# Routing constants ahead of the gate load, one group's transposes one unit later, last transposes ahead of logits

## The chip, the cores and the metric

The kernel runs on one NeuronCore of a Trainium2 chip. The metric is the device time of one execution in microseconds; the time shown is the median of three runs. The engines are named as in the profile: PE (TensorE, matmuls and transposes) with its weight loads PEld, DVE (VectorE), ACT (ScalarE), POOL (GpSimd), and SP (SyncE), whose queue issues almost all DMAs.

## The reference

Windowed attention over 4 batches of 576 tokens with 8 heads of 64, then a mixture of 8 experts with a fixed capacity of 288 tokens each, then a second MLP with a squared ReLU.

```python
# attention: 64-wide causal window
scores = scale * np.matmul(q, k.transpose(0, 1, 3, 2))
mask = (rel >= 0) & (rel < window)
attn = softmax(np.where(mask, scores, -1e9))
out = np.matmul(attn, v)
...
# moe: all (token, expert) logits in descending order; a token goes to its first expert with room
logits = x @ w_gate
for idx in np.argsort(-logits.flatten()): ...
out[mask] = np.maximum(x[mask] @ w1[e], 0.0) @ w2[e]
...
# moe2
h = np.maximum(x @ w_in, 0.0)
return (h * h @ w_out)
```

The order of all logits decides who gets which expert, so the first expert can start only when attention is through for every token.

## The kernel before, in words

Attention works on 18 units. A **group** n (0 to 5) is a third of the sequence (192 tokens) of two batches; each group has three units j of 64 queries. The units run in the order (0,0), (0,1), (0,2), (1,0) and so on, and step s of the main loop is a software pipeline over them:

- `scores` of unit s on PE (32 matmuls into the PSUM tile `sp`, of which there is one), then the masked maximum on DVE and the exponentials on ACT into `P` (`exps`);
- `ptr_` of unit s-1: PE transposes `P`, ACT copies the result to `PT`;
- `pump(s)`: the SP queue issues loads that fall due;
- `xtr` of unit s-2: transposes its output `X` for the gate logits;
- `pv` of unit s-1: 32 matmuls of `PT` with the value tiles `w`, then the division on DVE into `X`; a group's last unit also stores `X` to DRAM (`xs`);
- in every third step `logits` (gate logits of a whole group) and `turn` (they are transposed into `L`);
- `tr(n,h,p)`: a quarter of a group's keys and queries (batch h of the pair, head half p) is transposed on PE, 4 transposes of `kn` and 4 of `qn`, each of these into one of the four small PSUM tiles `pt`; DVE copies the keys to `KT`, ACT the queries to `QT`. The table `due` says in which step which quarter is transposed. Group 0 is done ahead of the loop, amid matmuls on the identity (`keep_warm`).

Keys and queries are loaded by `load_qk`, 8 DMAs for a group (16 half ones for group 0), each of 192 KB in pieces of 256 bytes; the order of all loads on SP is fixed by the list `loads`, and a load of SP has to wait for the semaphore of the eighth load ahead of it. For blocks that overlap, POOL copies half a value tile from the tile before (line 66).

`Routing.constants` (called through `between`) makes what the router needs: on POOL six iotas, two clears of 128x2304 half-precision tiles (`G`, `A_`, lines 295 and 296) and a triangle; on DVE one scaling of `tab` (line 293), which reads what POOL's iota wrote, and six small clears. Before, it is called at the end of step 6.

After attention come eight routing phases (DVE and PE in turn), which find each expert's tokens; the first gives the expert number that the first weight load waits for. The expert and MLP matmuls follow in an order that is fixed when the program is built.

Of the kernel before, what the change touches and what calls it, by code (L numbers as in the profile page):

```python
# [18 lines left out]
def A(t,off,dims):  # L19
    return bass.AP(tensor=t.tensor, offset=t.offset+off, ap=[list(d) for d in dims])  # L20

def attention(tc, nc, q,k,v,wgate, xs, L, identf, between=lambda: None, before_last=lambda: None, WARM=(8,4,4,4), NW=14):


    with ExitStack() as st:
# [12 lines left out]
        units=[(n,j) for n in range(6) for j in range(3)]  # L38
        N=len(units)
# [37 lines left out]
        def pump(s):  # L77
            while loads and loads[0][0]<=s:
                o,n,x=loads.pop(0)
                if x is None: load_qk(n)  # L80
                else: load_v(x,W(*x))
# [5 lines left out]
        def sel(out, kind):  # L87
            for h in range(2):
                o=out[64*h:64*h+64]
                if kind=="cur":  # L90
                    nc.gpsimd.affine_select(out=o,in_=o,pattern=[[-1,64]],compare_op=OP.is_ge,fill=NEG,base=0,channel_multiplier=1)
                else:
                    nc.gpsimd.affine_select(out=o,in_=o,pattern=[[1,64]],compare_op=OP.is_ge,fill=NEG,base=-1,channel_multiplier=-1)
        sel(MK[:,0,0],"cur"); nc.gpsimd.memset(MK[:,0,1],NEG)
        sel(MK[:,1,0],"prev"); sel(MK[:,1,1],"cur")
        for t in W_: nc.vector.memset(t[:,:,64:66],1.0)
        nc.sync.dma_start(wg[:,:,0:8], A(wgate,0,[[8,128],[128*8,4],[1,8]]))
        pump(-1)
        state={}
        def bank(shape):  # L100
            t=ps.tile([128,512],F32,name="pt",bufs=4)
            if len(shape)==1: return t[:,0:shape[0]]
            return t[:,0:shape[0]*shape[1]].rearrange("p (a b) -> p a b",b=shape[1])
        def tr(n, h, p):

            g=n//2
            if n not in QT: QT[n]=wk.tile([128,2,4,T3],F32,name="qt",bufs=2)
            ps_={}
            for nm in ("kn","qn"):
                ps_[nm]=bank((2,T3))  # L110
                for e in range(2):
                    hp=2*p+e
                    for c in range(2):
                        nc.tensor.transpose(ps_[nm][:,e,c*96:c*96+96],N_[nm,n,h][:,c,2*hp:2*hp+2,:].rearrange("p h d -> p (h d)"),identf[:96,:96])

            def out(t): return t.rearrange("p e (u c) -> p e c u",c=2)
            def inp(t): return t.rearrange("p e (c u) -> p e c u",c=2)
            nc.vector.tensor_copy(out(KT[:,batch(n,h),2*p:2*p+2,g*T3:(g+1)*T3]),inp(ps_["kn"]))
            nc.scalar.copy(out(QT[n][:,h,2*p:2*p+2]),inp(ps_["qn"]))
        def scores(u, hps=range(4), sp=None):  # L120

            n,j=u
            i=block(u)
            s0=64*max(i-1,0)
            if sp is None:
                sp=ps.tile([128,2,4,128],F32,name="sp",bufs=1)
                sp=[sp[:,r] for r in range(2)]
            if u not in state: state[u]=wk.tile([128,2,4,128],F32,name="P",bufs=2)
            P=state[u]
            for hp in hps:  # L130
                for r in range(2):
                    a=slice(64*r,64*r+64)
                    for h in range(2):
                        nc.tensor.matmul(sp[r][64*h:64*h+64,hp,:],QT[n][a,h,hp,64*j:64*j+64],KT[a,batch(n,h),hp,s0:s0+128],start=True,stop=True)
            return lambda: exps(u,hps,sp,P)
# [8 lines left out]
        def ptr_(u):  # L144
            P=state[u]
            PT=wk.tile([128,2,4,128],F32,name="PT")
            for r in range(2):
                pt=bank((4,128))
                for hp in range(4): nc.tensor.transpose(pt[:,hp,:],P[:,r,hp,:],identf)
                nc.scalar.copy(PT[:,r],pt)  # L150
            state[u]=PT
        X={}
        def pv(u):
            n,j=u
            PT=state[u]
            po=ps.tile([128,2,512],F32,name="po",bufs=1)
            pw=po[:,:,0:264].rearrange("p r (c d) -> p r c d",d=66)
            for r in range(2):
                for hp in range(4):
                    for h in range(2):  # L160
                        nc.tensor.matmul(pw[64*h:64*h+64,r,hp,0:65],PT[:,r,hp,64*h:64*h+64],W(n,h,j)[:,2*hp+r,0:65],start=True,stop=True)
            if j==0: X[n]=wk.tile([128,3,4,2,64],F32,name="X",bufs=2)
            den=wk.tile([128,2,4],F32,name="den")
            nc.vector.tensor_scalar(den,pw[:,:,:,64],1e-9,None,op0=OP.add)
            rc=wk.tile([128,2,4],F32,name="rc")
            nc.vector.reciprocal(rc,den)
            nc.vector.tensor_tensor(out=X[n][:,j].rearrange("p c r d -> p r c d"),in0=pw[:,:,:,0:64],in1=rc[:,:,:,None].to_broadcast([128,2,4,64]),op=OP.mult)
            if j==2:
                for h in range(2):
                    nc.sync.dma_start(A(xs,(batch(n,h)*S+(n//2)*T3)*512,[[512,64],[64*512,3],[1,512]]), X[n][64*h:64*h+64].rearrange("p j c r d -> p j (c r d)"))  # L170
            return po
        XT={}
        def xtr(u):
            n,j=u
            xp=bank((4,128))
            for hp in range(4): nc.tensor.transpose(xp[:,hp,:],X[n][:,j,hp].rearrange("p r d -> p (r d)"),identf)
            XT[u]=wk.tile([128,4,128],F32,name="XT",bufs=4)
            if u==units[-1]: nc.scalar.copy(XT[u],xp)
            else: nc.vector.tensor_copy(XT[u],xp)
        def logits(n):  # L180
            lp=bank((128,))
            for hp in range(4):
                for j in range(3): nc.tensor.matmul(lp[32*j:32*j+32,0:128],wg[:,hp],XT[n,j][:,hp],start=hp==0,stop=hp==3)
            nc.vector.tensor_copy(LT,lp[0:96,0:128])
        def turn(n):
            lt=bank((96,))
            nc.tensor.transpose(lt,LT,identf[:96,:96])
            nc.vector.tensor_copy(L[:,3*n:3*n+3,:],lt.rearrange("p (j e) -> p j e",e=32)[:,:,0:8])
        def logits_at_once(u, out):
            for hp in range(4): nc.tensor.matmul(out,XT[u][:,hp],wg[:,hp,0:8],start=hp==0,stop=hp==3)  # L190
# [9 lines left out]
            else: scores(units[0],range(2,4))()  # L200
        due={}
        for n in range(1,6):
            for x,z in zip(((0,0),(1,0),(0,1),(1,1)),(1,1,2,2) if n==1 else (0,1,1,2)): due.setdefault(3*n-3+z,[]).append((n,*x))
        for s in range(N):
            d=due.get(s,[])
            if s>0:
                then=scores(units[s])
                if s>3:
                    for x in d[:1]: tr(*x)
                    d=d[1:]  # L210
                ptr_(units[s-1])
                then()
            pump(s)
            if s>1: xtr(units[s-2])
            if s>0: pv(units[s-1])
            if s>4 and s%3==2: logits(s//3-1)
            for x in d: tr(*x)
            if s>5 and s%3==0: turn(s//3-2)
            if s==6: between()
        lt=ps.tile([128,2,4,128],F32,name="sp",bufs=1)[:,0,0]  # L220
        xtr(units[N-2])
        turn(4)
        logits_at_once(units[N-3],lt[:,0:8])
        ptr_(units[N-1])
        pv(units[N-1])
        logits_at_once(units[N-2],lt[:,8:16])
        xtr(units[N-1])
# [772 lines left out]
@with_exitstack  # L1000
def kernel(ctx, tc, q, k, v, wg, w1, w2, win, wout, out):
    nc=tc.nc
    cp=ctx.enter_context(tc.tile_pool(name="consts",bufs=1))
    dram=ctx.enter_context(tc.tile_pool(name="dram",bufs=1,space=bass.MemoryType.DRAM))
    ctx.enter_context(tc.manual_schedule())
    identf=cp.tile([128,128],F32,name="identf")
    make_identity(nc,identf)
    L=cp.tile([128,18,8],F32,name="L")
    xs=dram.tile([B*S,H*D],F32,name="xs")
    route=Routing(tc,nc,cp,L,Clock())  # L1010
    route.wk=ctx.enter_context(tc.tile_pool(name="rk",bufs=1))
    attention(tc,nc,q,k,v,wg,xs,L,identf,between=route.constants,before_last=lambda: list(route.prepare(slice(0,15))))
    FFN(ctx,tc,nc,route,identf,xs,w1,w2,win,wout,out).run()
# [29 lines left out]
```

## Time and profile before

| what | value |
|---|---|
| median of 3 runs | 851.94 us (851.27 to 854.9) |
| profiled execution | 851.18 us, of which the span from first to last instruction is 849.5 us |
| PE busy | 784.7 us, 92% of the span |
| DVE, ACT, POOL busy | 56%, 47%, 32% |
| attention, to the last logits' copy to `L` | until 119 us |
| DMA | 198 GB/s over the first 80 us, in which 15.86 of 104.89 MB move |

Read it so: PE is busy almost throughout, so the few stretches in which it waits are what a change in the order of instructions can move. Attention is the first seventh of the span, and the loads of keys, queries and values run beside nearly all of it. Times below are from the start of the span.

### The profile page before, as it was taken

What the parts mean: (1) busy time and instruction counts of PE and PEld (TensorE: products, weight loads), DVE (VectorE), ACT (ScalarE), POOL (GpSimd) and SP (SyncE); (2) the same over time, 40 slices, a digit from 0 to 9 for tenths busy, and PEclk for the clock granted to TensorE, in tenths of its full rate; (3) what the DMA queues carried; (4) which work ended last, traced back from release to release, by engine and by line L of the source; (5) the groups of instructions that cost most, each with busy time, mean ns of one, the idle gap of its engine ahead of it and who ended that gap; (6) DMA issues with size and microseconds to landing.
All of it is one profiled execution on the core that took longest, in us unless ns stands there. A gap on an engine that the chain in (4) does not pass through costs nothing.

```text
span 849.5 us, 16319 instructions
## 1 busy us (share of the span) xinstructions
PE 784.7 (92%) x6389; PEld 710.7 (84%) x6389; DVE 472.0 (56%) x1379; ACT 400.1 (47%) x777; POOL 268.7 (32%) x245
## 2 busy tenths in 40 slices
PE   7979964989898989699999999999999999999996
PEld 6768853978897878588899998878998999999995
DVE  3677878577468999587655446424123653121111
ACT  4657831323445654353354545444455454454432
POOL 1242004333443443333146552113123553121103
PEclk9889985898899999799999999999999999999998
DMA  9999225273755554662356551414212534111001
GB/s 172 197 215 197 58 64 128 100 148 134 172 212 186 192 205 162 142 211 25 95 192 157 171 196 54 63 65 78 94 56 100 182 144 148 49 50 51 1 1 74
DMA packets 95516, 104.89 MB, mean 123 GB/s; under 512 B 62160, under 2 KB 70352, under 8 KB 95440
## 3 DMA queue, kind: packets, MB, share of 16 engines
q1 hardware_dynamic: 92368, 94.41, 37.4%
q0 software_dynamic: 3072, 9.45, 7.0%
q8 instruction: 50, 0.82, 0.4%
q14 instruction: 26, 0.21, 0.1%
HBM read 86.01 MB, written 17.84 MB: 122 GB/s over the span
## 4 chain that ended last, share of the span: by engine, by line
PE 33%; issue 18%; POOL 3%; DMA 1%; DVE 0%; ACT 0%; POOLq 0%
PE acc L966 9%; PE l L947 8%; PE acc L852 8%; PE acc L894 7%; POOL wlo L690 2%; DMA xg<-xs,idx 1%; POOL out_dram L936 1%; PE rt L399 0%; PE acc L801 0%; PE rt L801 0%; PE rt L516 0%; DVE M L456 0%; PE rt L432 0%; DVE hlo L956 0%; POOLq L690 0%
## 5 line engine op out<-in xcount | busy, mean ns | idle before, releaser
L690 POOL TENSOR_TENSOR wlo<-wr,whi 128x512 fp32r<-128x512 f32 x95 | 148.2, 1578 | 275.2 <-ACT whi L677 249.4
L956 DVE TENSOR_TENSOR hlo<-h,hhi 128x384 fp32r<-128x384 f32 x96 | 57.6, 600 | 159.6 <-ACT hhi L954 159.6
L951 ACT ACTIVATE r<-l 128x384 f32<-128x384 f32 x93 | 45.7, 491 | 195.8 <-PE l L947 195.8
L947 PE MATMUL l<-yhi,wlo 128*128 128x384 f32 x372 | 127.6, 343 | 0.0
L947 PE MATMUL l<-yhi,whi 128*128 128x384 f32 x372 | 127.0, 341 | 0.3 <-ACT r L951 0.3
L947 PE MATMUL l<-ylo,whi 128*128 128x384 f32 x372 | 126.8, 341 | 0.0
L966 PE MATMUL acc<-whi,hlo 128*128 128x512 f32 x288 | 116.4, 404 | 2.5 <-DVE hlo L956 2.5
L966 PE MATMUL acc<-wlo,hhi 128*128 128x512 f32 x288 | 115.2, 400 | 0.0
L677 ACT CAST whi<-wr 128x1024 fp32r<-128x1024 f32 x96 | 99.7, 1049 | 30.7 <-DMA wr<-in_moe_w_dram 30.7
L966 PE MATMUL acc<-whi,hhi 128*128 128x512 f32 x288 | 114.0, 396 | 0.0
L690 DVE TENSOR_TENSOR wlo<-wr,whi 128x512 fp32r<-128x512 f32 x97 | 85.4, 888 | 24.8 <-ACT whi L677 24.6
L947 PEld LDWEIGHTS l<-yhi,whi 128*128 128x128 f32 x372 | 70.9, 191 | 5.0 <-ACT r L951 0.6
L690 POOL TENSOR_TENSOR wlo<-wt,whi 128x512 fp32r<-128x512 f32 x32 | 45.6, 1451 | 90.1 <-ACT whi L677 88.5
L947 PEld LDWEIGHTS l<-ylo,whi 128*128 128x128 f32 x372 | 70.6, 190 | 3.8
L852 PE MATMUL acc<-xhi,wlo 128*128 128x288 f32 x256 | 73.1, 298 | 0.0
L947 PEld LDWEIGHTS l<-yhi,wlo 128*128 128x128 f32 x372 | 70.5, 190 | 1.3 <-issue 1.2
L852 PE MATMUL acc<-xhi,whi 128*128 128x288 f32 x232 | 69.9, 301 | 0.0
L852 PE MATMUL acc<-xlo,whi 128*128 128x288 f32 x232 | 69.6, 300 | 0.0
L894 PE MATMUL acc<-hhi,whi 128*128 128x288 f32 x256 | 68.3, 300 | 0.0
L894 PE MATMUL acc<-hhi,wlo 128*128 128x288 f32 x256 | 67.6, 299 | 0.0
L894 PE MATMUL acc<-hlo,whi 128*128 128x288 f32 x256 | 67.3, 299 | 0.0
L966 PEld LDWEIGHTS acc<-whi,hlo 128*128 128x128 f32 x288 | 54.9, 190 | 13.9 <-DVE hlo L956 2.9
(194 smaller groups left out, 1484.4 us busy)
## 6 DMA issues: line engine op xcount, KB each, us to landing
wr<-in_moe_w_dram SPq DMA_DIRECT2D x32, 1024.0 KB, 5.5
wr<-conv SPq DMA_DIRECT2D x16, 1024.0 KB, 4.7
wr<-in_moe_w_in_dram SPq DMA_DIRECT2D x16, 512.0 KB, 4.6
wr<-in_moe_w_out_dram SPq DMA_DIRECT2D x16, 512.0 KB, 5.4
conv<-wt SPq DMA_DIRECT2D x16, 512.0 KB, 3.0
xs<-X SPq DMA_DIRECT2D x12, 384.0 KB, 4.4
kn<-in_k_dram SPq DMA_DIRECT2D x20, 192.0 KB, 4.7
qn<-in_q_dram SPq DMA_DIRECT2D x20, 192.0 KB, 5.1
```

What stands on the lines that cost most here:

```text
L677: nc.scalar.copy(hi,src)
L690: (nc.gpsimd if p else nc.vector).tensor_tensor(out=lo[:,s],in0=src[:,s],in1=hi[:,s].bitcast(F32),op=OP.subtract)
L852: nc.tensor.matmul(ps[f][:,:CAP],self.w[n0+kk][a][:,f*128:(f+1)*128],x[b][:,kk],start=c==0,stop=c==11)
L894: nc.tensor.matmul(p[:,:CAP],self.w[n0+4+k//2][a][:,o:o+128],h[k][b][:,:CAP],start=c==0,stop=c==23)
L936: st=nc.gpsimd.indirect_dma_start(out=self.out,out_offset=bass.IndirectOffsetOnAxis(ap=idt[:,t:t+1],axis=0),in_=ot,in_offset=None)
L947: nc.tensor.matmul(p[:,:HN],self.w[n0+f][a][:,kk*128:(kk+1)*128],y[half][b][:,kk],start=c==0,stop=c==11)
L951: nc.scalar.activation(r,p[:,:HN],AF.Relu); at=self.clk.aop(HN)
L956: nc.vector.tensor_tensor(out=h["lo"],in0=h2,in1=h["hi"].bitcast(F32),op=OP.subtract); self.clk.op(HN,t,0)
L966: nc.tensor.matmul(acc[3*half+t],h[b][:,t*128:(t+1)*128],w[a][:,512:1024],start=f==0 and c==0,stop=f==15 and c==2)
```

## The change

Three calls change their places; no instruction is added or removed.

```diff
         for t in W_: nc.vector.memset(t[:,:,64:66],1.0)
+        between()
         nc.sync.dma_start(wg[:,:,0:8], A(wgate,0,[[8,128],[128*8,4],[1,8]]))
...
-            for x,z in zip(((0,0),(1,0),(0,1),(1,1)),(1,1,2,2) if n==1 else (0,1,1,2)): due.setdefault(3*n-3+z,[]).append((n,*x))
+            for x,z in zip(((0,0),(1,0),(0,1),(1,1)),(2,2,2,2) if n==1 else (0,1,1,2)): due.setdefault(3*n-3+z,[]).append((n,*x))
...
             if s>5 and s%3==0: turn(s//3-2)
-            if s==6: between()
         lt=ps.tile([128,2,4,128],F32,name="sp",bufs=1)[:,0,0]
         xtr(units[N-2])
+        ptr_(units[N-1])
         turn(4)
         logits_at_once(units[N-3],lt[:,0:8])
-        ptr_(units[N-1])
         pv(units[N-1])
```

One line is added above, so a line of the changed kernel from 97 on to 219 has a number one higher than before.

On POOL, the constants stand now right behind the attention masks (`mk`) and ahead of the first value copies; this is the difference at that place.

```order
 L91 AFFINE_SELECT mk<-mk 64x64 x2
+L287 IOTA io_159 128x8
+L287 IOTA de_161 128x8
+L287 IOTA tab_163 128x32
+L287 IOTA tab 128x96
+L295 MEMSET G 128x2304
+L296 MEMSET A__170 128x2304
+L299 AFFINE_SELECT tri<-tri 128x128
+L287 IOTA tp 64x18 x2
+L287 IOTA tcn 128x18
 L66 COPY w_87<-w_85 64x8x64
```

The same ten instructions (two iotas share a row) stood between the sixteenth and the seventeenth value copy. On DVE, the changed kernel's start reads:

```order
14 L96 MEMSET w_98 128x8x2
15 L293 TENSOR_SCALAR tab<-tab 128x96
16 L297 MEMSET on 128x128
17 L298 MEMSET tri 128x128
18 L305 MEMSET asg 128x18
19 L306 MEMSET lim 128x8
20 L307 MEMSET kp 128x36
21 L308 MEMSET cum 128x1
22 L119 COPY kt<-pt 128x2x2x96 x2
```

Rows 15 to 21 are new there: the first key copies of group 0 (row 22) now stand behind the scaling of `tab`, which waits for POOL. On PE, before, two quarters of group 1 (four rows of line 114) stood ahead of the scores of unit 2:

```order
31 L161 MATMUL po<-w_86,PT 64x65
32 L114 MATMUL pt<-identf,kn 128x96 x4
33 L114 MATMUL pt<-identf,qn 128x96 x4
34 L114 MATMUL pt<-identf,kn 128x96 x4
35 L114 MATMUL pt<-identf,qn 128x96 x4
36 L134 MATMUL sp<-kt,qt 64x128 x16
37 L149 MATMUL pt<-identf,P 128x128 x8
38 L176 MATMUL pt<-identf,X 128x128 x4
39 L161 MATMUL po<-w_85,PT 64x65
```

Now step 2 runs up to its `pv` first, and all four quarters follow it; the scores behind them are those of unit 3, the first that read group 1:

```order
50 L162 MATMUL po<-w_86,PT 64x65
51 L115 MATMUL pt<-identf,kn 128x96 x4
52 L115 MATMUL pt<-identf,qn 128x96 x4
53 L115 MATMUL pt<-identf,kn 128x96 x4
54 L115 MATMUL pt<-identf,qn 128x96 x4
55 L115 MATMUL pt<-identf,kn 128x96 x4
56 L115 MATMUL pt<-identf,qn 128x96 x4
57 L115 MATMUL pt<-identf,kn 128x96 x4
58 L115 MATMUL pt<-identf,qn 128x96 x4
59 L135 MATMUL sp<-kt,qt 64x128 x16
```

The copies of DVE and ACT that go with the moved quarters move with them. On SP nothing moves. At the end of attention the transposes of the last unit's `P` go ahead of one `turn` and one unit's logits on PE.

## Rows read from the trace of the kernel before

**Rows 1.** The page, part 1: busy time (share of the span) and instructions.

```profile
PE 784.7 (92%) x6389; PEld 710.7 (84%) x6389; DVE 472.0 (56%) x1379; ACT 400.1 (47%) x777; POOL 268.7 (32%) x245
```

**Rows 2.** Windows by step: length, busy of each engine, granted clock, DMA share, GB/s.

```profile
14.33:25.16 10.83, 6.89 (x88) 4.80 (x88) 3.96 (x21) 4.44 (x13) 0.61 (x1) 0.85 1.13 201
25.16:31.87 6.71, 6.71 (x93) 6.03 (x93) 3.88 (x21) 3.97 (x12) 2.35 (x4) 0.73 1.03 200
51.49:61.23 9.74, 5.12 (x93) 4.53 (x93) 6.83 (x29) 4.34 (x14) 7.12 (x14) 0.91 1.07 200
61.23:68.85 7.62, 7.62 (x108) 6.85 (x109) 5.71 (x26) 4.86 (x15) 2.32 (x4) 0.67 0.91 218
73.33:78.38 5.05, 5.05 (x94) 4.53 (x93) 4.42 (x25) 4.42 (x14) 1.06 (x2) 1.00 1.08 205
78.38:83.65 5.27, 5.27 (x110) 4.66 (x109) 4.51 (x23) 4.46 (x14) 0.60 (x1) 1.00 0.85 217
```

**Rows 3.** Timeline of PE, first wait: start, duration, what [idle before it <-releaser].

```profile
17.85 0.30 PE L114 MATMUL pt<-identf,kn 96*128 96x96 f32 x1
...
24.49 0.74 PE L114 MATMUL pt<-identf,qn 96*128 96x96 f32 x3 [0.71 <-DMA qn<-in_q_dram]
...
31.87 1.54 PE L134 MATMUL sp<-kt,qt 64*64 64x128 f32 x32
```

**Rows 4.** Timeline of all engines around the routing constants.

```profile
54.91 0.14 POOL L287 IOTA io<- 128x8 f32 x1
...
55.35 2.04 POOL L295 MEMSET G<- 128x2304 f16 x1
...
55.45 3.93 DVE L293 TENSOR_SCALAR tab<-tab 128x96 f16<-128x96 f16 x1 [2.83 <-POOL tab L287]
...
55.93 3.46 DVE L118 COPY kt<-pt 128x384 f32<-128x384 f32 x1
...
57.30 2.04 POOL L296 MEMSET A__976<- 128x2304 f16 x1
...
61.23 1.99 PE L134 MATMUL sp<-kt,qt 64*64 64x128 f32 x32 [4.62 <-DVE mn L142]
```

**Rows 5.** Timeline of all engines at the program's start.

```profile
3.23 0.52 POOL L91 TENSOR_SCALAR_AFFINE_SELECT mk<-mk 64x64 f32<-64x64 f32 x2
...
7.06 0.56 DVE L118 COPY kt<-pt 128x384 f32<-128x384 f32 x1 [1.02 <-PE pt L114]
...
7.95 0.66 PE L134 MATMUL pt<-kt,qt 64*64 64x128 f32 x14 [0.23 <-ACT qt L119]
```

**Rows 6.** Line 52, the third group's last query load: issue and landing.

```profile
L52 SPq DMA_DIRECT2D qn<-in_q_dram x1: 570/570/570, 30.1 to 30.1; - x1
...
DMA to landing us min/median/max: 4.4/4.4/4.4
```

**Rows 7.** Line 52, the sixth group's last query load: issue and landing.

```profile
L52 SPq DMA_DIRECT2D qn<-in_q_dram x1: 569/569/569, 73.3 to 73.3; - x1
...
DMA to landing us min/median/max: 6.0/6.0/6.0
```

**Rows 8.** Timeline of PE: transposes that read these two loads.

```profile
38.15 0.49 PE L114 MATMUL pt<-identf,qn 96*128 96x96 f32 x4
...
89.54 0.49 PE L114 MATMUL pt<-identf,qn 96*128 96x96 f32 x4
```

**Rows 9.** Timeline of PE at the end of attention.

```profile
111.84 0.98 PE L190 MATMUL sp<-wg,XT 128*128 128x8 f32 x8
112.68 1.07 PE L149 MATMUL pt<-identf,P 128*128 128x128 f32 x8
114.03 1.24 PE L161 MATMUL po<-w,PT 128*64 128x65 f32 x32 [0.28 <-issue]
```

**Rows 10.** Timeline of DVE in the first dispatch, behind attention.

```profile
139.82 6.79 DVE L407 TENSOR_SCALAR lf<-li 128x18 f32<-128x18 int32 x1
```

**Rows 11.** Span and mean granted TensorE clock.

```profile
core 0: 849.5 us, clock 0.953
```

## The prediction

> **What bounds the kernel now.** I read the page's first part, then windows by step, then the timelines of the two steps that stand out. PE is busy for 92% of the span [rows 1], and behind attention the order on all engines is the same in both kernels, so the change is worth what PE waits in the first 119 us. The windows [rows 2] run from one unit's scores to the next. A regular step takes 5.05 us, or 5.27 us where it has logits, with PE busy all through at the full clock. Two places do not look like that. From 14.33 to 31.87, two steps take 10.83 and 6.71 us: PE is busy for 6.89 of the first, and the granted clock falls to 0.85 and 0.73. From 51.49 to 68.85, two steps take 9.74 and 7.62 us: busy for 5.12 of the first, the clock at 0.67 in the second. Meanwhile the DMAs carry about 200 GB/s at a share near 1 in every row, so loads land at the pace of the DMA engines, and PE being earlier will not bring them earlier.
>
> The first place is a wait for data: the second group's transposes start at 17.85, and the last of them waits until 24.49 for the last query load; the next group's scores come at 31.87 [rows 3]. The second is the routing constants [rows 4]: DVE's scaling of `tab` takes 3.93 us for 96 numbers and ends when POOL's two clears end, at 57.30 + 2.04 = 59.34. A key copy sits behind it for 3.46 us, the masked maxima behind that, and PE, which needs `sp` read, idles 4.62 us until 61.23.
>
> **The change, part by part.**
>
> Constants out of step 6: the two steps fall back to the regular ones. 9.74 - 5.05 = 4.69 us, and 7.62 - 5.27 = 2.35 us of low clock behind the wait, together **-7.0 us** [rows 2]. If only the wait went and the low clock stayed, -4.7; more than 7.0 has no source there.
>
> Constants into the start: POOL ends its masks at 3.23 + 0.52 = 3.75 [rows 5]; from the first iota to the end of `A_` it took 59.34 - 54.91 = 4.43 us [rows 4], so it ends at about 8.2. DVE's `tab` scaling is held until then as it was before, and the six small clears behind it I count with it. Two key copies of 0.56 us follow, until 9.3, and the scores that began in bulk at 7.95 begin at 9.4 [rows 5]: **+1.45 us** at this place. From below it is nothing (DVE gets through between the two clears), from above some 2 us (the longer clear once more). POOL's value copies and the gate load are not held: the first waits for data until later, the second for a clear ahead of the constants. Queued behind DVE's wait are the key copies, then the first scores on PE. What hides the 1.45 us is the next part's wait for data; without that cover it would count in full.
>
> Second group's transposes one step later: the scores, `P` transposes, `X` transposes and `pv` of step 2 now fill the wait. That is less than a regular step, so from 17.85 + 1.45 = 19.3 it ends before 19.3 + 5.05 = 24.35, as the last query lands (24.49). All four quarters then stand in a row with four PSUM tiles between them. The slowest behind them is DVE with four key copies of 0.56 us, from about 24.5 until 26.7; I take unit 3's scores to start at 26.8 (an estimate), 5.1 us earlier than 31.87 [rows 3]. Not all of it can be kept. The third group's last query load is issued at 30.1 and lands 4.4 us later, at 34.5 [rows 6]; its transposes ran at 38.15 [rows 8] and would run at 33.1. They wait: the gain is cut to 38.15 - 34.6 = **-3.5 us**. By the same cut, the +1.45 us and any error up to 1.6 us in my 26.8 cost nothing, which is why I don't add the start. Bounds: -2 (unit 3's scores only at 28.4 or later) and -5.1 (the load lands 1.6 us earlier).
>
> How far the loads let PE run ahead: groups four and five land with more room than this. The sixth group's last query load is issued at 73.3 and lands at 79.3 [rows 7]; its transposes ran at 89.54 [rows 8], and 10.5 us earlier is 79.0. **+0.3 us**, between 0 and 1.
>
> Last transposes ahead of logits: PE has the `turn` and 0.98 us of logits between `X` and `P` transposes, and idles 0.28 us before the last `pv` while ACT copies `PT` [rows 9]. In the new order those logits stand in ACT's copy time. The work is the same, so only the idle 0.28 us goes: **-0.3 us** (0 to -0.3: PE's work ahead of `pv` ended at 114.03 - 0.28 = 113.75, so it cannot start sooner).
>
> Here is a rule that speaks against the change. The row first: after the wait for loads, the clock stood at 0.73 for the mean of a step [rows 2], that is at 1.2 GHz for part of it. The Trainium skill, TensorE: Matmul & The Clock Gate, section "HAM oscillation — how this bites in real kernels", says that an array which gets short bursts of work between waits for DMA falls back to the low clock and starts each burst cold. The changed kernel keeps a wait for the second group, shorter, and gets a new one of over a microsecond for the third. By that rule the low clock comes back behind them, and the 2.35 us return: 843.7 us instead of 841.4. By the rows I expect the full clock, since the steps at 1.00 are those in which PE works through, and between the two short waits it does.
>
> **The sum**: -7.0 - 3.5 + 0.3 - 0.3 = -10.5 us. The profiled execution took 851.18 us (849.5 us of span and 1.7 around it), 0.76 below the median, so 840.7 for it and **841.4 us** for the median.
>
> **The rivals.**
>
> Low clock behind the remaining waits: one stretch as in the second place costs 2.35 us [rows 2]. Against it: both waits are under 2 us by the sums above. About 843.7; two such stretches, or loads that land 2 us later against PE, 844 to 846.
>
> The transfer was the limit anyway. The DMA share is near 1 in every step of rows 2, so if the last loads of attention set its end, the change does nothing: 852. Against it: the value and key loads are through by then, and the sixth group has 89.54 - 79.3 = 10.2 us of room [rows 7, 8], which is my cap.
>
> More than forecast: a 6.79 us hold of DVE in the first dispatch [rows 10], over a conversion of 18 numbers, has the form of the one in rows 4. Should the shift let DVE in ahead of POOL there, up to some 5 us more go: 836. Against it: what leads up to it is in the same order and moves as a whole.
>
> Slower: the clock after attention. The mean grant is 0.953, so 0.047 / 0.5 x 849.5 = 80 us ran at the low level [rows 11], most of it behind attention. A microsecond of low clock cost about 2.35 / 5 = 0.47 us in the second place. To lose the 10.5 us and another 4.3, PE would have to spend 14.8 / 0.47 = 31 us more at 1.2 GHz in the expert stages: about 856. For it speaks only that the stages start at another moment; against it that their work and its order are unchanged.
>
> **How the numbers follow.** Forecast (839.5 to 842.7) 0.66; low clock or later loads (842.7 to 846) 0.16; more than forecast (835 to 839.5) 0.08; less than a third of the gain, by loads or a hold at the start that is not covered (847.7 to 852 and over) 0.06; slower by over 0.5% 0.04. A difference of 0.5%, 4.3 us, is about what a measurement of this kernel can tell from none. The range is 838 to 845: it leaves out the tail of the third case, the end of the second and all of the last two, 0.2 in all. Faster is the first three cases, 0.90; the same 0.06; slower 0.04.
>
> **What would show it.** Step 7 from scores to scores at 5.05 us and no PE idle for DVE there; `tab` held at the start until about 8.2, the first key copies behind it; the first unit's scores in bulk at about 9.4; unit 3's scores near 27; the third group's query transposes waiting for a load until 34.6; the sixth group's beginning near 79; unit 17's logits in `L` at about 108.5 instead of 119. I am wrong if the clock is at 1.2 GHz anywhere between 10 and 105 us, if the loads land later than before, or if the time from that copy to the end differs from before by more than a microsecond.

## The result, and the profile after

The changed kernel takes 842.38 us (median of 4 runs, 840.86 to 846.04); before took 853.27 us beside it (851.27 to 854.9). The ratio on record is 0.9885, with an interval of 0.9849 to 0.9922; the two medians alone would give 0.9872. That is 1.1% faster, and inside the predicted range. Its profiled execution took 841.97 us. These are its busy line, first, and its span and mean granted clock, second (against [rows 1, 11]):

```profile
PE 779.5 (93%) x6389; PEld 706.3 (84%) x6389; DVE 470.8 (56%) x1379; ACT 400.7 (48%) x777; POOL 270.1 (32%) x245
```

```profile
core 0: 840.2 us, clock 0.961
```

The windows by step of the changed kernel, each from one unit's scores to the next, with the columns of [rows 2]:

```profile
18.87:26.61 7.74, 6.78 (x112) 5.94 (x108) 6.21 (x27) 6.48 (x19) 0.00 (x0) 1.00 1.04 194
26.61:31.45 4.84, 4.84 (x85) 4.10 (x84) 3.51 (x21) 3.33 (x10) 2.35 (x4) 1.00 1.00 211
31.45:41.14 9.69, 7.26 (x93) 6.09 (x93) 4.30 (x23) 5.04 (x15) 2.31 (x4) 0.82 1.24 181
...
50.85:55.90 5.05, 5.05 (x93) 4.53 (x92) 4.42 (x25) 4.43 (x14) 1.88 (x4) 1.00 0.92 210
55.90:61.66 5.76, 5.61 (x109) 4.60 (x108) 4.57 (x23) 4.79 (x15) 1.32 (x3) 1.00 1.12 193
...
71.18:76.94 5.76, 5.61 (x109) 4.60 (x109) 4.57 (x23) 4.80 (x15) 1.56 (x3) 1.00 1.03 183
```

Two things differ from the two bad places of before. The steps of units 7 and 8 take 5.05 and 5.76 us at the full clock, where they took 9.74 and 7.62. And the wait of the second group is shorter, but the step of unit 4 now takes 9.69 us, at a clock of 0.82. The timeline of PE in the changed kernel shows why:

```profile
24.89 0.47 PE L115 MATMUL pt<-identf,qn 96*128 96x96 f32 x3 [0.67 <-DMA qn<-in_q_dram]
...
26.61 1.36 PE L135 MATMUL sp<-kt,qt 64*64 64x128 f32 x32
...
33.47 0.47 PE L115 MATMUL pt<-identf,kn 96*128 96x96 f32 x3 [0.68 <-DMA kn<-in_k_dram]
34.81 0.27 PE L115 MATMUL pt<-identf,qn 96*128 96x96 f32 x1 [0.88 <-DVE mn L143]
35.96 0.47 PE L115 MATMUL pt<-identf,qn 96*128 96x96 f32 x3 [0.87 <-DMA qn<-in_q_dram]
36.26 1.53 PE L150 MATMUL pt<-identf,P 128*128 128x128 f32 x8
37.59 1.06 PE L177 MATMUL pt<-identf,X 128*128 128x128 f32 x4
38.57 1.83 PE L162 MATMUL po<-w,PT 128*64 128x65 f32 x32
...
41.14 1.10 PE L135 MATMUL sp<-kt,qt 64*64 64x128 f32 x32
...
42.89 1.04 PE L150 MATMUL pt<-identf,P 128*128 128x128 f32 x8
43.77 0.60 PE L177 MATMUL pt<-identf,X 128*128 128x128 f32 x4
44.30 1.15 PE L162 MATMUL po<-w,PT 128*64 128x65 f32 x32
```

Unit 3's scores start at 26.61 (31.87 before), then, behind unit 4's scores at 31.45, the third group's loads hold the transposes three times, 2.43 us together (7.26 busy of 9.69). The profile puts the second wait down to DVE; in a later trace of this kernel the same row starts at 34.80, just behind its load, which landed at 34.66. Behind these waits `P` transposes, `X` transposes and `pv` take 1.53, 1.06 and 1.83 us, where they take 1.04, 0.60 and 1.15 in the next step: 1.63 us for the low clock. Unit 5's scores come at 41.14; they came at 41.77 before. Of 5.26 us won, 0.63 is left.

The account, from start times in both timelines: unit 5's scores -0.63; units 7 and 8 -6.55; unit 11 +0.49 (5.76 for 5.27); the tail, from unit 17's scores to the first routing matmul, -0.48 (12.42 for 12.90). No run has the new order of the last calls alone, but over all traces of this document this tail takes 12.41 to 12.57 us in six of the seven with that order (13.24 in the other) and 12.89 to 13.72 in the seven with the old one. Routing starts at 112.05 instead of 119.22, **-7.17 us**. From there to the end of the span it takes 728.19 us instead of 730.26, **-2.07** more.

The start of the changed kernel, POOL's and DVE's timelines, against [rows 5]:

```profile
4.25 2.05 POOL L295 MEMSET G<- 128x2304 f16 x1
6.21 2.05 POOL L296 MEMSET A__170<- 128x2304 f16 x1
```

```profile
4.37 3.93 DVE L293 TENSOR_SCALAR tab<-tab 128x96 f16<-128x96 f16 x1 [3.02 <-POOL tab L287]
5.92 2.38 DVE L119 COPY kt<-pt 128x384 f32<-128x384 f32 x1
...
8.31 0.56 DVE L119 COPY kt<-pt 128x384 f32<-128x384 f32 x1
```

The hold moved here whole: 3.93 us for 96 numbers again, ending with the second clear (8.26 on POOL, 8.30 on DVE). The first key copy ends with it, and the second at 8.87. Beside them, ACT's second query copy and PE's weight loads for the bulk of the first scores:

```profile
7.92 0.50 ACT L120 COPY qt<-pt 128x384 f32<-128x384 f32 x1 [1.08 <-PE pt L115]
...
8.98 0.45 PEld L135 LDWEIGHTS pt<-kt,qt 64*64 64x64 f32 x14 [0.30 <-issue]
```

The query copy ends at 8.42, the key copy at 8.87, and the scores follow the key copy: the hold delays them by some 0.45 us in this trace.

### The profile page after: what moved, and what is told of

Read it like the earlier page. It is cut to its first block, busy times and chain, and to the rows that moved or that the text cites. A ratio compares the mean times of both kernels' runs of the same rounds, so it can differ in the third digit from the quotient of the medians.

```text
span 840.2 us, 16316 instructions
## 1 busy us (share of the span) xinstructions
PE 779.5 (93%) x6389; PEld 706.3 (84%) x6389; DVE 470.8 (56%) x1379; ACT 400.7 (48%) x777; POOL 270.1 (32%) x245
## 4 chain that ended last, share of the span: by engine, by line
PE 32%; issue 18%; POOL 3%; DMA 2%; DVE 1%; ACT 0%; POOLq 0%
PE acc L966 9%; PE l L947 8%; PE acc L852 8%; PE acc L894 6%; POOL wlo L690 2%; DMA xg<-xs,idx 1%; POOL out_dram L936 1%; DMA wr<-conv 1%; PE rt L399 1%; PE acc L801 0%; PE rt L432 0%; PE rt L516 0%; PE rt L801 0%; POOL xg L788 0%; DVE M L456 0%
## 5 line engine op out<-in xcount | busy, mean ns | idle before, releaser
L690 DVE TENSOR_TENSOR wlo<-wr,whi 128x512 fp32r<-128x512 f32 x97 | 83.2, 865 | 25.8 <-ACT whi L677 25.4
```

Source lines behind the costliest of these rows:

```text
L690: (nc.gpsimd if p else nc.vector).tensor_tensor(out=lo[:,s],in0=src[:,s],in1=hi[:,s].bitcast(F32),op=OP.subtract)
```

## The experiments

Some kernels have a time of one execution only. Such single times scatter by some 10 us, those of before too (850.42 to 861.17 in 17 runs on one chip, 846.65 for a single one at another time), so these kernels are read by their traces.

**One part alone: constants.** Before, with only this edit:

```diff
         for t in W_: nc.vector.memset(t[:,:,64:66],1.0)
+        between()
...
-            if s==6: between()
```

> Only the constants move to the start; the transposes and the last calls stand as before. Attention's end is read at the first counting matmul of the router (before 119.2 us, changed kernel 112.1). Theory 1 (the parts add, and the delay at the start is hidden by the wait for the second group's queries): steps 7 and 8 together 10.8 instead of 17.4 us, the first scores in bulk 1.0 us later, unit 2's scores at 25.2 as before, end at 112.6, time some 6.6 us below before. Theory 2 (the delay at the start is not hidden): unit 2's scores at 26.2 and the end at 113.6. In both, no low clock between 45 and 110 us.

846.71 us against 856.55, ratio 0.9877 (0.9814 to 0.9939). Windows of this kernel: up to unit 2's scores, then the steps of units 2, 7 and 8:

```profile
14.00:25.02 11.02, 6.64 (x98) 4.67 (x91) 4.79 (x29) 5.18 (x15) 0.61 (x1) 0.95 1.12 196
25.02:32.70 7.68, 7.68 (x94) 6.83 (x93) 3.73 (x21) 4.54 (x12) 2.35 (x4) 0.63 1.07 197
52.32:57.37 5.05, 5.05 (x94) 4.53 (x93) 4.42 (x25) 4.42 (x14) 2.69 (x5) 1.00 0.98 211
57.37:63.13 5.76, 5.61 (x109) 4.60 (x109) 4.58 (x23) 4.79 (x15) 0.28 (x1) 1.00 1.05 196
```

Unit 2's scores stand at 25.02 (25.16 before): the hold at the start is hidden by the wait for loads. Units 7 and 8 take 10.81 us instead of 17.36. Routing starts at 114.82, 4.4 us earlier than before (112.6 was expected). It would be more but for unit 2's step (7.68 us for 6.71, at a clock of 0.63 for 0.73), unit 11 (0.49) and the last logits, which ran at the low clock (1.88 us, 1.06 in the changed kernel). The measured gain is that of the whole change.

**The other part alone: transposes.** Before, with only this edit:

```diff
-...(1,1,2,2) if n==1 else (0,1,1,2)): ...
+...(2,2,2,2) if n==1 else (0,1,1,2)): ...
```

> Only the second group's transposes move; the constants stay in step 6 and the last calls as before. Theory 1 (the third group's loads land near 36 us whatever PE does, and the low clock follows from the wait for them): unit 3's scores at 26 to 27, unit 5's at 40.5 to 41.2, so that little of 5 us is left, and the end at 118.5. Theory 2 (the loads landed late in the changed kernel because of the constants at the start; here they land near 34.5 as before): unit 5's scores at 38.3, the end at 115.7. Rival to both (the wait costs no clock): unit 5's scores at 39.5.

855.94 us against 856.55, ratio 0.9999 (0.9966 to 1.0032): no gain. The window of unit 4's step, and two places of the timeline:

```profile
33.50:40.87 7.37, 5.27 (x93) 4.56 (x93) 4.45 (x23) 4.27 (x13) 0.97 (x2) 1.00 1.06 169
```

```profile
37.27 0.47 PE L114 MATMUL pt<-identf,qn 96*128 96x96 f32 x3 [2.10 <-DMA qn<-in_q_dram]
...
57.54 3.93 DVE L293 TENSOR_SCALAR tab<-tab 128x96 f16<-128x96 f16 x1 [5.82 <-POOL tab L287]
...
63.31 1.98 PE L134 MATMUL sp<-kt,qt 64*64 64x128 f32 x32 [7.61 <-DVE mn L142]
```

Unit 3's scores came at 28.38 (26 to 27 expected): PE waited for the second group's last query load until 25.76. The third group's last query load takes most of what was left: unit 5's scores are at 40.87, and unit 7's at 50.59, each 0.9 us ahead of before's. This wait of 2.10 us has no low clock behind it, unlike the waits in the changed kernel: the whole step was granted 1.00. The stall in step 7 takes the rest and more: unit 8's scores are at 63.31, 2.1 us *behind* before's 61.23, since DVE waits for POOL's `tab`, and POOL does not come earlier because PE does.

**What sets that stall: the clears taken out of it.** Before, with the two clears (`G`, `A_`) at the start and the other constants still at the end of step 6:

```diff
         for t in W_: nc.vector.memset(t[:,:,64:66],1.0)
+        clears()
...
-        self.G=t([128,18,128],F16,"G"); g.memset(self.G,0.0)
-        self.A_=t([128,18,128],F16,"A_"); g.memset(self.A_,0.0)
```

> The kernel before with only POOL's two clears moved to the start; iotas, the scaling of tab and DVE's small clears stay at the end of step 6. Theory 1 (the stall of step 7 is DVE held by the two clears and nothing else): steps 7 and 8 together at 10.8 to 11.3 instead of 17.4 us, scaling of tab under 0.3 us, no low clock behind it, first scores in bulk at 7.95 as before. Theory 2 (the wait of DVE for POOL's iotas, 2.8 us of idle DVE ahead of the scaling, is part of the stall, as POOL's value copies ahead of them wait for loads): steps 7 and 8 together at 13 us or more.

850.87 us in one execution (before 854.69). The timeline of all engines, at the start and in step 7:

```profile
5.76 2.02 POOL L287 MEMSET A__161<- 128x2304 f16 x1
5.91 0.56 DVE L119 COPY kt<-pt 128x384 f32<-128x384 f32 x1 [4.56 <-PE pt L115]
7.61 0.56 DVE L119 COPY kt<-pt 128x384 f32<-128x384 f32 x1 [1.14 <-PE pt L115]
```

```profile
56.33 0.61 POOL L66 COPY w<-w 64x512 f32<-64x512 f32 x1 [0.16 <-DMA w<-in_v_dram]
56.90 0.14 POOL L292 IOTA io<- 128x8 f32 x1
...
57.44 0.19 DVE L298 TENSOR_SCALAR tab<-tab 128x96 f16<-128x96 f16 x1 [4.12 <-POOL tab L292]
...
60.21 1.20 PE L135 MATMUL sp<-kt,qt 64*64 64x128 f32 x22 [2.89 <-DVE mn L143]
```

Without clears behind it the scaling takes 0.19 us, not 3.93: the hold was theirs. Yet the two steps still take 14.88 us (17.36 before, 10.81 without any constants). The rest of the stall is a queue: POOL makes `tab` only behind a value copy, which waits for a value load, and DVE waits 4.12 us. This trace does not show which of the two is larger, since its value load landed late, at 56.21 (54.22, 54.77 and 55.26 in three traces of before). In those three, DVE waited 2.83, 3.51 and 2.65 us for `tab`, and the scaling then took 3.74 us longer than here; PE's wait was 4.62, 5.30 and 4.44 us, which is the sum of the two less 1.95 us each time. So in the unchanged kernel the hold was the somewhat larger part. At the start, two key copies that read PSUM take 0.56 us each, the first of them wholly while `A_` is cleared: they are not held. In the changed kernel the first key copy's 2.38 us was its place behind the scaling.

**The hold at the start taken away.** The changed kernel, with the scaling of `tab` behind group 0's transposes:

```diff
-        v.tensor_scalar(self.tab,self.tab,0.5,None,op0=OP.mult)
...
             else: scores(units[0],range(2,4))()
+        scale()
```

> The changed kernel with DVE's scaling of tab moved behind group 0, so that it no longer stands ahead of the first key copies; all else of the constants stays at the start. Theory 1 (it is the scaling alone that POOL's clears hold, and the key copies are held only by standing behind it): the first scores in bulk at 7.9 to 8.0 as in the kernel before instead of 8.5 to 9.0; unit 3's scores at 26 to 27 as in the changed kernel, since the second group's queries land no earlier, so nothing at the end of attention. Theory 2 (POOL's clears hold the key copies too): the first scores stay at 8.5 or later. Theory 3 (the delay at the start was not hidden): unit 3's scores about 0.8 us earlier, near 25.8, and the end of attention with them.

843.48 us in one execution. Its timeline has, at the start:

```profile
5.92 0.56 DVE L119 COPY kt<-pt 128x384 f32<-128x384 f32 x1 [4.19 <-PE pt L115]
...
9.14 0.66 PE L135 MATMUL pt<-kt,qt 64*64 64x128 f32 x14 [0.23 <-ACT qt L120]
```

The key copy is free. Yet the bulk of the first scores starts at 9.14, no earlier than with the hold (7.9 to 8.0 was expected), and unit 2's scores are at 18.99 against 18.87. The start of this execution was late for another reason: the second quarter's key transposes ran at 7.73, where they ran at 7.06 in the changed kernel and at 6.52 before, and the scores follow them by 1.41 us here and by 1.43 before, behind ACT's query copy. With the hold they cannot start before the second key copy ends at 8.87. So the hold costs what the loads leave of it: some 0.45 us in the first trace of the changed kernel, nothing in its second one, whose transposes ran at 7.75.

**More room for the third group.** The changed kernel, with that group's transposes one step later too:

```diff
-...(2,2,2,2) if n==1 else (0,1,1,2)): ...
+...(2,2,2,2) if n==1 else (1,1,2,2) if n==2 else (0,1,1,2)): ...
```

> The changed kernel with the third group's transposes one step later too (steps 4 and 5 instead of 3, 4 and 5). Theory 1 (what was given back between unit 4's and unit 5's scores, 9.7 us instead of 5.05, is the wait for the third group's loads and the low clock behind it): both go, unit 5's scores at 37.5 to 38.5 instead of 41.1, then up to 1 us is given back to the fourth and the sixth group's loads, end at 108.5 to 109.5 instead of 112.1. Theory 2 (the loads of the later groups cap it, as little room is left there): the wait moves to the fourth group, end at 111 to 112.

846.79 us against 856.55, ratio 0.9893 (0.9843 to 0.9942). Two rows of its timeline:

```profile
37.21 1.10 PE L135 MATMUL sp<-kt,qt 64*64 64x128 f32 x32
...
142.26 0.90 PE L801 MATMUL acc<-identf,xg 96*128 96x96 f32 x4 [1.90 <-DMA xg<-xs,idx]
```

Unit 5's scores come at 37.21, 3.93 us ahead of the changed kernel, and routing starts at 109.49 (112.05). So the wait for the third group's loads is what took the gain. In this execution it was lost again behind attention: from routing to the first expert matmul 35.70 us, not 33.28, with a wait for a gather, and from routing to the end 734.0 us, not 728.2. Both kernels were timed once more, on one chip:

> The changed kernel once more. If the wait for the third group's loads and the low clock behind it belong to the change: unit 5's scores between 40 and 42 again. If they were the luck of one execution: near 38.3. The time again 1.0 to 1.3% below the kernel before.

> The changed kernel with the third group's transposes one step later, once more and on the same chip as the changed kernel. Theory 1 (its 2.5 us at the end of attention are real and were lost behind it by a late gather in that one execution): end of attention at 108.5 to 109.5, from there 33.3 us to the first expert matmul as in the other kernels, time 2 to 3 us below the changed kernel's. Theory 2 (what attention gains is always lost behind it): 35 us and more from the end of attention to the first expert matmul again, and no difference in time.

845.58 us for the changed kernel, ratio 0.9893 (0.9869 to 0.9916); 843.96 for the variant, ratio 0.9883 (0.9856 to 0.9911). Routing started at 113.59 and 110.29, the first expert matmul 33.40 and 33.45 us later, so the extra wait behind attention did not recur. The variant is 3.3 us ahead at routing in the trace and 1.6 us in the median; the intervals overlap, so it is not shown to be faster. The changed kernel's second trace has the lost time in both places:

```profile
26.14 0.47 PE L115 MATMUL pt<-identf,qn 96*128 96x96 f32 x3 [1.91 <-DMA qn<-in_q_dram]
...
37.49 0.47 PE L115 MATMUL pt<-identf,qn 96*128 96x96 f32 x3 [2.00 <-DVE mn L143]
```

The second wait is put down to DVE, but these transposes read a load that landed at 37.45.

**The clock in that wait.** The changed kernel, with 24 more matmuls on the identity ahead of the third group's transposes in step 4:

```diff
+                    if s==4:
+                        for wb in [bank((128,)) for _ in range(4)]:
+                            for _ in range(6): nc.tensor.matmul(wb,identf,identf,start=True,stop=True)
```

> The changed kernel with 24 matmuls on the identity, some 3.2 us at the full clock, between unit 4's scores and the third group's transposes that wait for loads there; they compute nothing that is used. Theory 1 (the low clock from 36.7 to 40.1 follows from PE standing still in the wait): the clock stays at 2.4 GHz, the steps behind run at their regular length, unit 5's scores at 39.3 to 39.8 instead of 41.1, end 1.5 us earlier, at 110.5. Theory 2 (the low clock has another cause, such as the number of transposes): the clock falls as before, and unit 5's scores at 41 or later.

849.39 us against 856.55, ratio 0.9929 (0.9884 to 0.9975). On PE's timeline:

```profile
33.05 5.62 PE L212 MATMUL pt<-identf 128*128 128x128 f32 x48
...
42.47 1.10 PE L135 MATMUL sp<-kt,qt 64*64 64x128 f32 x32
```

The low clock was gone until 112 us, so it did come from the waits. But the filler (24 matmuls, two rows each) took 5.62 us and not the 3.2 that were expected. It ends at 38.67, after the load has landed (37.11), and unit 5's scores are no earlier: what the clock gives, the filler takes.

**Why the loads land later.** Two traces of before, unchanged, a third of the changed kernel, and before with 24 such matmuls ahead of the second group's transposes in steps 1 and 2:

```diff
+            if s in (1,2):
+                for wb in [bank((128,)) for _ in range(4)]:
+                    for _ in range(6): nc.tensor.matmul(wb,identf,identf,start=True,stop=True)
             for x in d: tr(*x)
```

> The kernel before, unchanged, for the landing of the third group's last query load, beside the changed kernel on the same chip. Theory 1 (the moved transposes let the loads land later): 34.5 to 35.1 us here, as in the trace of before (34.57) and in the two kernels that left the transposes where they were (34.9 and 35.1). Theory 2 (landings just scatter from one execution to the next): a value between 34.5 and 37.5 here as well.

> The same kernel once more, for the scatter: theory 1 as in the first of the two, within 0.5 us of it; theory 2 differs from it by a microsecond or more, or lies above 35.5.

> The changed kernel a third time. Theory 1: the third group's last query load lands at 35.9 us or later, as in its two traces so far (about 35.9 and 37.45), and unit 5's scores start at 41 us or later. Theory 2: it may land at 34.6 to 35.1, and unit 5's scores start at 40 or earlier.

> The kernel before with 24 matmuls on the identity into the four small PSUM tiles ahead of the second group's transposes in steps 1 and 2, so that PE works in the wait for the loads while no DVE or ACT copy moves (the extra matmuls are no part of the computation and change no output). If PE being busy is what lets loads land later, the third group's last query load lands at 35.9 or later; if not, at 34.5 to 35.1, and it is left to the copies of DVE and ACT or to scatter. The granted clock should stay at 1.00 between 20 and 32 us, and the time within 3 us of before's.

The times were 851.1, 852.54, 842.55 and 850.17 us. The landing of the third group's last query load (issue and time to landing, from the rows of its line; where the record is missing, the end of PE's wait for it):

| transposes | landing, us |
|---|---|
| as before, 5 traces | 34.57, 34.75, 34.93, 35.06, 35.55 |
| second group moved, 6 traces | about 35.9, 35.93, about 36.2, 37.11, 37.23, 37.45 |
| second and third moved, 2 traces | 35.11, 35.19 |
| as before, PE kept busy, 1 trace | 36.27 |

The scatter within a row of the table is 1 to 1.5 us, so single landings prove little. The second unchanged trace, at 35.55, lies above the 35.5 that was set as a sign of mere scatter; still, the first two sets do not overlap. PE's activity alone can do it, by the one trace of the last row; then it is odd that the third row is early. The cause stays open. The filler has another lesson. Windows of its units 2, 7 and 8, and DVE's timeline:

```profile
25.83:36.29 10.46, 10.46 (x142) 9.94 (x141) 4.62 (x23) 4.45 (x12) 2.35 (x4) 1.00 0.95 182
55.71:62.29 6.58, 5.12 (x93) 4.52 (x92) 6.50 (x29) 4.33 (x14) 6.19 (x13) 1.00 1.07 194
62.29:67.56 5.27, 5.27 (x108) 4.64 (x108) 5.13 (x26) 4.66 (x15) 0.49 (x1) 1.00 0.70 188
```

```profile
56.75 3.70 DVE L296 TENSOR_SCALAR tab<-tab 128x96 f16<-128x96 f16 x1
57.33 3.13 DVE L118 COPY kt<-pt 128x384 f32<-128x384 f32 x1
```

Here PE reaches unit 7 at 55.71, 4.2 us later than before, and leaves the stall at 62.29, only 1.1 us later; with no low clock behind it, routing starts at 118.01, ahead of before. In all six traces with constants in step 6 (one of them without the clears), unit 8's scores lie between 60.2 and 63.3, while unit 7's lie anywhere from 50.6 to 55.7. The stall ends by POOL's time. In the first of the two further traces of the unchanged kernel POOL's rows read:

```profile
54.89 0.61 POOL L66 COPY w<-w 64x512 f32<-64x512 f32 x1 [1.08 <-DMA w<-in_v_dram]
55.46 0.14 POOL L287 IOTA io<- 128x8 f32 x1
```

In five of the six traces this copy starts 0.12 us behind the landing of a value load, also where the profile puts its wait down to PE; in the sixth that landing is not recorded.

## Why the prediction was right, and where it was not

The total was right: -10.5 us predicted, -9.2 in the span of the two traces, and the median near the top of the forecast's own band. Its parts were less so. All three things by which I said that I would be wrong were there: a stretch at 1.2 GHz (36.26 to 40.40), loads that land later, and a time behind attention that differs by more than a microsecond.

- **Constants out of step 6**, -7.0: measured -6.55. The mechanism was only half told. I put the stall on the clears' hold, 3.74 us beyond the scaling's own 0.19. DVE's wait of 2.83 us for POOL's `tab` behind value copies, which [rows 4] show too, I left out; the kernel without the clears still lost 4 of the 6.5 us, in an execution in which that wait was 4.12. The amount held because the move takes both away. The missing 0.5 us is unit 8's step, 5.76 instead of 5.27: `P`'s second half waits for ACT's query copy. Step 11 pays the same.
- **Constants into the start**, +1.45, hidden: hidden, as one part alone shows, but there was less to hide. The bulk of the first scores started at 8.98 instead of 7.95, and of that only some 0.45 is the hold; the rest is transposes that ran later. I counted two key copies behind the hold, and it was one: the first ends with the scaling, as the copy in [rows 4] does (55.93 + 3.46 = 59.39).
- **Second group's transposes**, -3.5: measured -0.63, outside the bounds of -2 and -5.1. This is the step that failed: the lower bound allowed for late scores of unit 3, not for late loads. Unit 3's scores came at 26.61 (26.8 forecast). The cut by the third group's load was right in kind, but I took the landing of before, 34.5, as fixed, and the waits as too short to cost clock. The load landed at 35.9, and the low clock took 1.63 us. What was left was 0.63 us at unit 5, and in the other two traces of the changed kernel 41.10 and 42.69 against 41.65 and 42.99 in the unchanged ones. So the condition of the first rival, low clock or later loads, was met, and in all three traces of the changed kernel: unit 4's step was granted 0.81 to 0.83. I gave it 2.35 us and a chance of 0.16; the low clock cost 1.63. The rule that I set against the rows is that of the Trainium skill, TensorE: Matmul & The Clock Gate, section "HAM oscillation — how this bites in real kernels": short bursts between waits for DMA run at the low clock. The changed kernel's trace agrees, with 0.59 granted from 36.26 to 40.40; the trace of the transposes alone does not, with 1.00 behind a wait of 2.10 us.
- **Sixth group's load**, +0.3: no wait, 0. **Tail**, -0.3: measured -0.48, a little beyond the bound of -0.3.
- **Behind attention**, 0: measured -2.07, more than the microsecond that I allowed. Nothing was changed there. From routing to the end, three traces of the changed kernel take 728.2 to 730.3 us and three of before 729.4 to 730.3, and all 14 traces, with the same work there, 728.2 to 734.0. So most of this is scatter, in the right direction by chance. DVE's row of 6.79 us stayed ([rows 10]): the rival "more" did not come.

So the median was met in part by luck: -3.5 was 2.9 too good, and the part behind attention was 2.1 too poor. The gain shown is that of the constants: alone they give 0.9877, the transposes alone 0.9999, both together 0.9885, and the intervals do not tell the first and last apart. The traces credit the transposes and the last calls together with 1.2 to 2.8 us beside the constants (routing at 112.05 to 113.59 against 114.82). Of that 0.8 is the low clock at the end of the constants' trace and 0.5 the last calls, so for the transposes between nothing and 1.5 us is left.

## What to carry to other kernels

A gain ahead of a stall is worth what is left of it behind the stall: first ask which engine's work ends the stall, and whether that work moves with your edit; here it went by value loads and POOL, so PE's earlier arrival bought nothing until the stall was removed. When work is pulled ahead of a load, do not take the load's old landing time as a constant: leave a microsecond or two, and price the wait with and without a low clock behind it: the runs here have both. A long instruction on DVE or POOL may be a hold by its neighbour: take the neighbour away before you explain the whole wait by it, and look at what that engine waited for ahead of it.

## What the runs showed of the hardware

- DVE's scaling of 96 half-precision numbers in SBUF took 0.19 us without POOL's clears behind it and 3.93 us with two of them, in step 6 and at the start alike; DVE's copies from PSUM took 0.56 us during a clear. The Trainium skill, SBUF — State Buffer, section "Who interferes with whom", says of a DVE instruction that takes the port pair shared with GpSimd that whoever issues first has the pair for the whole instruction and the other blocks; the traces agree that it blocks, but the hold lasted through two clears in a row. A row of the same form is that of line 407, 6.79 us again in the changed kernel. It ends as POOL's work beside it ends (139.44 and 139.41), but no run took that work away, so that it is a hold is not shown. DVE's row is first and POOL's second:

```profile
132.65 6.79 DVE L407 TENSOR_SCALAR lf<-li 128x18 f32<-128x18 int32 x1
```

```profile
133.27 6.14 POOL L690 TENSOR_TENSOR wlo<-wr,whi 128x512 fp32r<-128x512 f32 x5
```

- Behind three waits for loads, 2.43 us together, the clock stood at 1.2 GHz for most of 4.14 us (0.59 granted); behind a single one of 2.10 us, in the kernel with the transposes alone, it stayed at 2.4 GHz. With filler matmuls in place of the three it stayed at 2.4 GHz to the end of attention, and nothing was gained by it.
- A load of 192 KB took from 4.1 to 6.6 us to land at the same place of the same queue, and which order of PE's work went with which end of that was not explained.
